# The output product of a memory-recurrent attention in column pieces: one kernel, one change

## The chip, the cores and the metric

The kernel runs on one core of a Trainium2 chip. The metric is the device time of one execution in microseconds; the median of the runs counts. Lower is better. The engines are TensorE (PE, its weight loads PEld), VectorE (DVE), ScalarE (ACT), GpSimd (POOL) and the queue of SyncE (SP), which issues nearly all DMAs. Each engine works through its own instructions in order and waits on semaphores.

## What is computed

Two attentions read the same x (2048 rows of 512) and are mixed by a gate. A goes through 64 segments of 32 rows. Each segment sees 8 memory rows ahead of its own, and the memory rows that it puts out are the next segment's. B is an attention in four blocks of 512 with a linear memory. The reference, cut to what matters:

```python
for s in range(n_seg):                       # 64 segments, seg_len = 32, M = 8
    xs = x[:, s * seg_len:(s + 1) * seg_len, :]
    h = jnp.concatenate([mem, xs], axis=1)   # 40 rows
    q = jnp.einsum('btd,dhe->bhte', h, Wq)   # H = 32 heads of 128; k and v likewise
    ...
    p = _softmax(jnp.where(mask, scores, -1e9), axis=-1)
    o = jnp.einsum('bhqk,bhke->bhqe', p, v)
    o = jnp.einsum('bhte,hed->btd', o, Wo)   # 4096 -> 512
    mem = o[:, :M, :]                        # goes into the next segment
    outs.append(o[:, M:, :])
...
out = g * a + (1 - g) * b                    # g = sigmoid((x * gate_w).sum(-1))
```

## The kernel before

The program first computes B's projections for the first three blocks (up to 50 us of the profiled execution), while the weights of A arrive. Then a part follows, here called the memory part, in which the 64 segments run one after the other, and the rest of B's work fills the gaps.

A segment has 40 rows, and TensorE works on 32 columns of weights by four side by side. So the kernel takes 32 rows as the segment's own: the 8 memory rows and the first 24 rows of x (tile `hT`, the copy of the 24 rows by POOL in `x_copy`, L1555). The last 8 rows of four segments do not depend on the memory and are handled together as one "left" group of 32 rows (`xL`, `left_units`, 16 groups). Keys, queries and values of a left group are put beside those of its segments.

A tile of TensorE of 32 output columns (`pb[bk][SEG * j:SEG * (j + 1)]`, j = 0 to 3) is called a column tile here; four matmuls on the four column tiles run side by side. The steps of a segment are units with short names in a list:

- `K0x K0y K1x ... V1y`: projections (`proj`, L1305), half of the heads (b = 0, 1) and half of the contraction each: 8 matmuls of 512 columns. `k0 q0 v0 ...` evict them (`evac`, L390 on ScalarE or L392 on VectorE), `TK`, `TQ` turn keys and queries on VectorE (`flip`, L1317).
- `S` scores (L1598, L1603), `X` exponential on ScalarE (L1612), `Y` mask on VectorE (L1616), `M` sums (L1633), `L` reciprocal as logarithm and exponential on ScalarE (L1640, L1643), `N` normalization on VectorE (L1647), `n` that of the left columns on POOL (L1653).
- `PV0 PL0`, `PV1 PL1`: value products of each half of the heads, 16 matmuls of 40 columns (L1663) and 4 over the left rows (L1675). They use four row tiles of 32 contraction rows (`tile_position=(SEG * j, 0)`), and each half takes four PSUM banks. `E0a E0b E1a E1b` evict them into `OT_sb`.
- `W0a ... W1b`: product with Wo (`out_part`, L1392). Column tile j takes the heads 4k + j, all 512 outputs each, so that the four tiles hold four partial sums over 8 heads each.
- `H0`, `H1`: eviction of the partial sums as f32 (`WF`), `F0`, `F1`: a product with the f32 matrix `fold` (L1410) that adds the four partial sums and turns the result, so that features lie along the partitions. `hm` copies the 8 memory columns into the next `hT`, `ax` the other columns into `aT_st`.
- The left groups have `ol` units (the same product over `OTL`, 16 of them) and `of` (fold). `os` turns `aT_st` on VectorE and stores it (`aTd`), and the tail units `tb`, `tf` load 128 finished rows, mix them with B's and write them out.

Among these stand B's units: `bS` scores (L933, row tiles too), `bE` exponential (L954), `bP` value products (L986), `bT` what comes after them, `pj`, `pp` late projections of the last block.

The order of the work is written out: sixteen lists `A_LIST0` to `A_LIST15`, one for each four segments. A unit appends its instructions to its engines' streams when its name comes up; semaphore waits follow from what is read and written. A `~` behind a name swaps ScalarE and VectorE in its eviction. Names that end in `e` end a unit begun earlier. PSUM banks are given out in the order of the list (`Banks`), and a bank's new writer waits for its last reader. DMAs stand in SP's queue in the same order.

Of the kernel before, what the change touches and what calls it, by code (L numbers as in the profile page):

```python
# [42 lines left out]
class Banks:  # L43
# [3 lines left out]
    def __init__(self, res):  # L47
        self.free = list(range(len(res)))
        self.res = res
        self.oldest = True  # L50
        self.relief = lambda: False

    def take(self, long=False):
        while not self.free and self.relief():
            pass
        assert self.free, "out of banks"
        f = self.free
        if long:
            c = [b for b in f if b < 2] or f
        elif self.oldest:  # L60
            c = [b for b in f if b > 1] or f
        else:
            whole = [b for b in f if b > 1 and b ^ 1 in f]
            c = [b for b in f if b not in whole and b > 1] if len(whole) <= 4 else [b for b in f if b > 1]
            c = c or [b for b in f if b > 1] or f
        b = c[0]
        f.remove(b)
        return b

    def pair(self):  # L70

        found = lambda: [(max(self.free.index(b), self.free.index(b + 1)), b) for b in self.free if b % 2 == 0 and b + 1 in self.free]
        while not found() and self.relief():
            pass
        c = found()
        c = [x for x in c if x[1] > 1] or c
        assert c, "no two neighbouring banks"
        b = min(c)[1]
        self.free = [k for k in self.free if k not in (b, b + 1)]
        return [b, b + 1]  # L80
# [177 lines left out]
def build(nc, es, A_x, A_mem0, A_Wq, A_Wk, A_Wv, A_Wo, B_wq, B_wk, B_wv, B_wo, B_beta, gate_w, out, dbg=None):  # L258
# [31 lines left out]
    def alloc(stack, *specs):  # L290
        at, spans = 0, {}
        for name, shape, dt, n in specs:
# [10 lines left out]
    alloc(es, ("ident", [128, 128], BF16, 0), ("xT", [128, C, S], BF16, 0), ("hT", [128, C, SEG], BF16, 2),  # L303
          ("Wk_sb", [128, C, HE], BF16, 0), ("Wq_sb", [128, C, HE], BF16, 0), ("Wv_sb", [128, C, HE], BF16, 0),
          ("Wo_sb", [128, H, DM], BF16, 0), ("woB_sb", [128, C, DM], BF16, 0),
          ("gw_sb", [128, C], BF16, 0), ("g_sb", [128, NTT], F32, 0), ("omg_sb", [128, NTT], F32, 0),
# [6 lines left out]
          ("aTg", [128, C, 128], BF16, 0), ("fold", [128, SEG], F32, 0), ("VNL", [128, 2, 512], BF16, 0),  # L313
          ("WF", [128, DM], F32, 0))
# [6 lines left out]
    v.x_sb = v.Wo_sb[:, 0:NTT, :]  # L321
    v.wvB = v.woB_sb
# [7 lines left out]
          ("oTt", [128, 16, 32], F32, 0), ("t1_sb", [128, DM], F32, 0), ("aT_st", [128, C, 128], BF16, 2))  # L330
# [11 lines left out]
    dram("aTd", [NG, 128, DM])  # L342
# [4 lines left out]
    def Rs(name):  # L347
        if name not in R:
            R[name] = Res(name)
            home = v.home(name)  # L350
            if home:
# [5 lines left out]
             ("QT", "QT_sb"), ("VN", "V_sb"), ("Pn", "P_sb"), ("P0", "P_sb"), ("P1", "P_sb"), ("R0", "R_sb"), ("R1", "R_sb"), ("OTL", "OTL"),  # L357
             ("OT", "OT_sb"), ("oTt", "oTt"), ("t1", "t1_sb"), ("aT", "aT_st"))

    def late_home(name):  # L360
        if name.startswith(("aTd", "aTg", "PT")):
            return None
        h = next((t for p, t in homes if name.startswith(p)), None)
        if h in ("KTL", "QTL", "VL", "OTL"):
            h += name[len(h)]
        return h + name[3] if h == "aT_st" else h
# [27 lines left out]
    v.g_out = [P.group("out%d" % i, "out") for i in range(NG)]  # L394

# [32 lines left out]
    v.BK.oldest = False  # L428
    v.BK.free = sorted(v.BK.free)
    plan_a(v, NSEG_RUN)  # L430
    for go in v.g_out:
        if go.count:
            P.ops["sp"].append(Op("sp", (lambda go=go: (lambda sp: sp.wait_ge(go.sem, 16 * (go.base + go.count))))(), [], "final_wait_" + go.name))
# [7 lines left out]
def plan_const(v):  # L441
# [29 lines left out]
    def late():  # L471
# [7 lines left out]
        rf = Rs("fold")  # L479
        gp(lambda g: g.memset(v.fold[:], 0.0), rf, "fold0", True)  # L480
        for j in range(4):
            sel(v.fold[:], [[-1, SEG]], ALU.not_equal, 1.0, -SEG * j, 1, rf, "fold1_%d" % j)
# [17 lines left out]
def plan_warm(v):  # L500
    P, Rs, BK = v.P, v.Rs, v.BK
    v.warm = v.WF[:, :].bitcast(BF16)[:, 0:512]
# [12 lines left out]
def plan_loads(v, A_x, A_mem0, A_Wq, A_Wk, A_Wv, B_wq, B_wk, B_wv, B_wo, B_beta, gate_w):  # L515
# [35 lines left out]
    def wo(q):  # L551
        P.dma(v.grp("Wo%d" % (q // 2)), lambda s: s.dma_start(v.Wo_sb[:, 4 * q:4 * q + 4, :], wosrc[:, 4 * q:4 * q + 4, :]),
              writes=[Rs("Wo%d" % (q // 2))] + ([Rs("x_sb%d%d" % (q, h)) for h in range(2)] if q < 4 else []), name="dma_Wo%d" % q)
# [70 lines left out]
def gate_parts(v):  # L624
# [4 lines left out]
    def dots(k):  # L629
# [4 lines left out]
        def f_gate(pe):  # L634
            ins = None
            for i in range(4 * k, 4 * k + 4):
                for c in range(C):
                    ins = pe.matmul(v.pb[bk][:, i:i + 1], v.xT[:, c, i * 128:(i + 1) * 128], v.gw_sb[:, c:c + 1],
                                    start=(c == 0), stop=(c == C - 1), skip_group_check=True)
            return ins  # L640
        P.op("pe", f_gate, reads=x_res(v, k) + [Rs("gw")], writes=[v.rbank[bk]], name="gate_mm%d" % k)
        if k == NTT // 4 - 1:
            sigmoid(v, v.pb[bk][:, 0:NTT], v.g_sb, v.omg_sb, "g", [v.rbank[bk]])
            BK.give(bk)

    def memory():
# [8 lines left out]
        v.evac("dve", v.hT[0][:, :, 0:v.M], v.pb16[bk][:, 0:C * v.M].rearrange("p (c t) -> p c t", t=v.M), [bk], [Rs("hTm0_0"), Rs("hTm0_1")], "memT0")  # L655
# [133 lines left out]
class LateB:  # L789
# [25 lines left out]
    def project(self):  # L815
# [23 lines left out]
        P.op("pe", f, reads=x_res(v, v.NB - 1) + [Rs("wvB" if m == "V" else "woc%d" % (k % 4))], writes=[v.rbank[bk]], name="lp%d_%d" % (k, half))  # L839
# [4 lines left out]
    def finish(self):  # L844
# [9 lines left out]
        if k == 0:  # L854
            P.op("gp", lambda g: g.memset(self.vst[:, :, 16:17], 1.0), writes=[Rs("t1")], name="v17l")
# [3 lines left out]
                  self.vst[:, :, 0:16].rearrange("p (e m) d -> p m e d", e=2), "t1", "vd%d_%d" % (sb, i)),  # L859
# [9 lines left out]
class BAttn:  # L869
# [45 lines left out]
    def scores(self):  # L915
# [8 lines left out]
        bks = v.BK.pair() + v.BK.pair()  # L924
# [134 lines left out]
A_LIST0 = """  # L1059
    ixl wl 0.Q0x iKL0x iQL1x iQL0x 0.K0x 0.Q0y iQL0 0.K1x 0.K1y 0.q0 0.TQ0 iKL0 0.xc iQL0e 0.K0y iKL0e~ iKL1x 0.k1 bS wl bE bE bE iQL1 wl bE 0.k0~ iKL1 pj  # L1060
    iQL1e 0.qt 0.TK1 iVL1x iVL1 iVL0x iVL0 xl bP iVL0e pj bP iKL1e~ 0.TK0 0.Q1x iVL1e~ QL0x pp QL0 QL0e wl 0.Q1y bS VL0x wl bE VL0 0.V0x wl wl pj iVLt
    0.q1~ bE 0.S0 bE pj KL1x 0.TQ1 bE 0.X0 0.Y0 0.S1 KL0x 0.X1 0.Y1 bP wl 0.V0y VL0e~ 0.M1 0.v0 bP 0.L1 0.N1 0.M0 KL1 KL0 pp VL1x VL1 KL1e KL0e~ bS 0.n1
    pj pj 0.L0 0.N0 QL1x QL1 0.n0 VL1e~ bE bE 0.V1x 0.V1y bE QL1e bE 0.v1~ 0.PV0 1.qt 0.PL0 0.E0a 0.E0b~ 1.xc pj bP 0.PV1 0.PL1 0.E1a~ 0.W0b 0.E1b~ 0.W0a
    0.oL 0.W1a bT 0.W1b pp 0.H0~ bP bS 0.F0 0.H1~ bE 0.hm0 0.ax0 pj 0.F1 0.hm1~ 1.Q0x 1.K0x 1.K0y bE bE 1.k0 0.ax1~ 1.TK0 1.Q0y 1.q0~ 1.TQ0 bE 1.K1x 1.K1y
    1.Q1x 1.Q1y 1.k1 bP 1.TK1 1.S0 1.q1 1.TQ1 1.X0 1.Y0 1.V0x 1.V0y 1.v0 pp 1.S1 1.X1 1.Y1 1.M0 1.V1x 1.V1y 1.L0 1.n0 2.qt 1.N0 1.M1 1.L1 bP 1.n1 pj 1.v1
    1.N1 1.PV0 2.xc 1.PL0 1.E0b~ 1.E0a pj 1.PV1 pp 1.PL1 1.E1b~ 1.E1a~ 1.oL 1.W0a 1.W0b 1.W1b 1.W1a 1.H0 bS 1.F0 bE 1.hm0 1.H1~ 1.F1 2.Q0x 2.K0x 1.hm1~
    1.ax1 2.K0y 2.k0~ 2.TK0 2.Q0y 2.K1x 2.K1y 2.Q1x bE 2.Q1y bE bE 2.q0~ 2.TQ0 2.S0 bP 1.ax0 bP 2.k1~ 2.TK1 2.q1 2.TQ1 2.X0 2.Y0 bS 2.V1x 2.V1y 2.S1 bT
    2.M0 bE VLt bE 2.X1 2.Y1 2.V0x 2.V0y 2.L0 2.n0 2.N0 2.v0~ pj 2.v1 2.M1 2.L1 2.n1 2.N1 3.qt pj 2.PV0 2.PL0 2.E0b~ 2.E0a bE pj pj 2.PV1 2.PL1 2.E1a~ pp
    pp 2.E1b~ 2.oL 2.W0a 2.W0b bT bE 2.W1a 2.W1b 2.H0 3.xc bS bP 2.H1~ bP 2.F0 2.hm0 2.F1 3.K0x 2.ax0 3.Q0x bE bE 2.hm1~ 3.Q0y 3.K0y bE 2.ax1~ bE 3.q0
    3.k0 3.TQ0 3.K1x 3.K1y 3.TK0 3.Q1x 3.S0 3.X0 3.Q1y 3.q1 3.V0x 3.k1~ 3.TK1 3.Y0 3.TQ1 3.V0y 3.v0 3.M0 3.L0 3.n0 3.N0 3.V1x 3.S1 3.V1y bP 3.X1 3.Y1 bP  # L1070
# [813 lines left out]
```

## Time and profile before

| what | us |
|---|---|
| runs | 831.55, 832.46, 835.6 (median 832.46) |
| span of the profiled execution, from its first to its last instruction | 828.9 |
| PE busy | 804.7 |
| DVE busy | 575.6 |
| ACT busy | 592.2 |
| POOL busy | 287.6 |

The profile is of one execution. Of that execution the instruction span is recorded, 828.9 us; the time of a run also holds what lies around the instructions. Matmuls are pipelined: a matmul's recorded time runs from its first read to a modelled end, and matmuls that follow each other overlap. How fast TensorE works is therefore read from the distance between starts. A row of the profile's groups gives line, engine, operation, tiles written and read, shapes, count, busy time, the mean time of one in ns, and the idle time before them with what ended it.

### The profile page before, as it was taken

The page shows a single profiled execution, that of the slowest core. Times are in us where ns is not written, and L with a number is a line of the kernel's source. Part 1 is how long each engine was busy: PE and PEld are TensorE (multiplying, and loading weights), DVE is VectorE, ACT ScalarE, POOL GpSimd, SP SyncE. Part 2 cuts the span into 40 slices and gives each one's busy share as a digit, 9 for nine tenths or more (in the row PEclk, how much of TensorE's full clock was granted, in tenths as well). Part 3 has the DMA queues.
Part 4 walks back from the last instruction along what each step waited for, and adds up shares of the span by engine and source line. Part 5 has one row for each costly group of instructions (what it writes and reads, how often), then busy time and mean ns, then how long its engine had stood idle before and what let it go on. Part 6 is the DMA issues. An engine that isn't in the chain of part 4 may idle for free.

```text
span 828.9 us, 49046 instructions
## 1 busy us (share of the span) xinstructions
PE 804.7 (97%) x21947; PEld 433.6 (52%) x21947; DVE 575.6 (69%) x1392; ACT 592.2 (71%) x1510; POOL 287.6 (35%) x780
## 2 busy tenths in 40 slices
PE   8998999999999999999999999999999999999998
PEld 4544555555445555555555555554555555555544
DVE  4555666577677777687777777877777777677656
ACT  5557777777776867777777777677777686777654
POOL 4613333433333333434342333433333333334111
PEclk9999999999999999999999999999999999999999
DMA  8997312212011121111102121211102111210111
GB/s 329 419 374 223 87 36 62 47 26 60 19 38 36 31 50 27 44 37 47 38 19 46 30 50 32 47 38 46 37 21 50 27 49 33 47 36 17 43 27 47
DMA packets 98257, 57.48 MB, mean 69 GB/s; under 512 B 71800, under 2 KB 92160, under 8 KB 96512
## 3 DMA queue, kind: packets, MB, share of 16 engines
q1 hardware_dynamic: 97488, 53.58, 22.3%
q8 instruction: 172, 2.82, 1.4%
q10 hardware_dynamic: 560, 0.79, 0.3%
q14 instruction: 37, 0.30, 0.1%
HBM read 37.14 MB, written 17.20 MB: 66 GB/s over the span
## 4 chain that ended last, share of the span: by engine, by line
PE 81%; ACT 7%; DMA 5%; DVE 3%; issue 1%; POOL 1%; SPq 0%; ACTq 0%; DVEq 0%; POOLq 0%
PE ps L1305 44%; PE ps L1392 17%; PE ps L1410 4%; PE ps L1663 3%; PE ps L933 2%; PE ps L986 2%; DMA scr_mzd<-MZ 2%; PE ps L1505 2%; DMA scr_kqd<-stgk 2%; PE ps L1598 2%; PE ps L1633 1%; ACT PT L954 1%; PE ps L699 1%; ACT R_sb L1643 1%; ACT WF L390 1%
## 5 line engine op out<-in xcount | busy, mean ns | idle before, releaser
L960 POOL TENSOR_SCALAR_AFFINE_SELECT PT<-PT 128x128 bf16<-128x128 bf16 (+2 forms) x320 | 117.3, 367 | 204.5 <-ACT PT L954 163.5
L954 ACT ACTIVATE PT<-ps 128x512 bf16<-128x512 f32 x320 | 176.1, 609 | 5.8 <-PE ps L933 3.9
L1305 PE MATMUL ps<-Wq_sb,hT 128*32 128x512 bf16 x2048 | 139.4, 379 | 0.5
L1305 PE MATMUL ps<-Wv_sb,hT 128*32 128x512 bf16 x2048 | 137.6, 379 | 0.1
L1305 PE MATMUL ps<-Wk_sb,hT 128*32 128x512 bf16 x2048 | 136.9, 379 | 0.2
L1392 PE MATMUL ps<-Wo_sb,OT_sb 128*32 128x512 bf16 x2048 | 127.4, 380 | 0.0
L1653 POOL TENSOR_TENSOR P_sb<-P_sb,R_sb 128x64 bf16<-128x64 bf16 x128 | 50.9, 398 | 144.8 <-ACT R_sb L1643 140.9
L390 ACT ACTIVATE OT_sb<-ps 128x320 bf16<-128x320 f32 x167 | 67.9, 434 | 22.8 <-PE ps L1675 21.7
L1305 PEld LDWEIGHTS ps<-Wk_sb,hT 128*32 128x32 bf16 x2048 | 59.7, 97 | 45.8 <-ACT hT L390 2.6
L1305 PEld LDWEIGHTS ps<-Wq_sb,hT 128*32 128x32 bf16 x2048 | 59.3, 97 | 45.8 <-ACT hT L390 2.3
L1317 DVE STREAM_TRANSPOSE QT_sb<-QN_sb 128x256 f32<-128x256 f32 x128 | 56.1, 440 | 24.2 <-ACT QN_sb L390 22.0
L1392 PEld LDWEIGHTS ps<-Wo_sb,OT_sb 128*32 128x32 bf16 x2048 | 48.1, 96 | 45.7 <-ACT OT_sb L390 6.4
L1317 DVE STREAM_TRANSPOSE KT_sb<-KN_sb 128x256 f32<-128x256 f32 x128 | 55.9, 439 | 21.6 <-ACT KN_sb L390 18.8
L390 ACT ACTIVATE QN_sb<-ps 128x512 bf16<-128x512 f32 x83 | 49.9, 602 | 28.4 <-PE ps L1305 27.5
L390 ACT ACTIVATE WF<-ps 128x256 f32<-128x256 f32 x97 | 32.8, 381 | 51.6 <-PE ps L1392 51.5
L1612 ACT ACTIVATE P_sb<-ps 128x224 bf16<-128x224 f32 x128 | 45.9, 360 | 27.8 <-PE ps L1603 17.2
L390 ACT ACTIVATE KN_sb<-ps 128x512 bf16<-128x512 f32 x79 | 47.0, 599 | 25.7 <-PE ps L1305 24.8
L1305 PEld LDWEIGHTS ps<-Wv_sb,hT 128*32 128x32 bf16 x2048 | 50.7, 95 | 27.6 <-issue 1.3
L392 DVE CAST OT_sb<-ps 128x320 bf16<-128x320 f32 x89 | 42.9, 488 | 26.0 <-PE ps L1675 25.5
L392 DVE CAST V_sb<-ps 128x512 bf16<-128x512 f32 x82 | 55.9, 683 | 4.0 <-PE ps L1305 3.1
L1647 DVE TENSOR_TENSOR P_sb<-P_sb,R_sb 128x160 bf16<-128x160 bf16 x128 | 42.2, 329 | 20.1 <-ACT R_sb L1643 18.4
L1663 PEld LDWEIGHTS ps<-P_sb,V_sb 32*128 32x128 bf16 x2048 | 23.0, 91 | 54.4 <-DVE P_sb L1647 27.9
(139 smaller groups left out, 1484.7 us busy)
## 6 DMA issues: line engine op xcount, KB each, us to landing
Wk_sb<-in_A_Wk_dram SPq DMA_DIRECT2D x4, 1024.0 KB, 9.8
Wq_sb<-in_A_Wq_dram SPq DMA_DIRECT2D x4, 1024.0 KB, 13.7
Wv_sb<-in_A_Wv_dram SPq DMA_DIRECT2D x4, 1024.0 KB, 16.6
Wo_sb<-in_A_Wo_dram SPq DMA_DIRECT2D x8, 512.0 KB, 6.1
scr_vld<-VNL SPq DMA_DIRECT2D x16, 256.0 KB, 2.3
VL<-scr_vld SPq DMA_DIRECT2D x64, 64.0 KB
scr_kqd<-stgk SPq DMA_DIRECT2D x12, 256.0 KB, 9.6
Vj<-scr_vd SPq DMA_DIRECT2D x32, 68.0 KB, 2.4
```

Source lines behind the costliest of these rows:

```text
L390: P.op("act", lambda a: a.activation(dst, src, ACT.Copy), reads=[v.rbank[k] for k in bks], writes=dres, name=name)
L392: P.op("dve", lambda d: d.tensor_copy(dst, src), reads=[v.rbank[k] for k in bks], writes=dres, name=name)
L954: P.op("act", lambda a: a.activation(pt, v.pb[bk], ACT.Exp, scale=v.SCALE_B), reads=[v.rbank[bk]], writes=[rp], name="be%d_%d" % (n, t))
L960: P.op("gp", lambda g: g.affine_select(mv, mv, [[0, len(cut)], [1, 128]], ALU.is_ge, 0.0, base=0, channel_multiplier=-1), reads=[rp], writ ...
L1305: ins = pe.matmul(pb[bk][SEG * j:SEG * (j + 1), :], lhs(c), cols(w, j) if split else w[:, 512 * j:512 * (j + 1)], start=(c == 0), stop=(c ...
L1317: P.op("dve", lambda d: d.transpose(to, src), reads=reads, writes=writes, name=name)
L1392: ins = pe.matmul(pb[bk][SEG * j:SEG * (j + 1), :], lhs(4 * k + j), Wo_sb[:, 4 * k + j, :], start=(first and k == ks[0]), stop=False, skip ...
L1410: ins = pe.matmul(pb[bk][SEG * j:SEG * (j + 1), SEG * n:SEG * (n + 1)], cols, v.fold[:, :], start=True, stop=True, skip_group_check=True)
L1612: P.op("act", lambda a: a.activation(P_sb[:, b, :], pb[bk][:, 0:224], ACT.Exp, scale=SCALE), reads=[rbank[bk]], writes=[Rs("P%d" % b), Rs( ...
L1647: P.op("dve", lambda d: d.tensor_tensor(wide(P_sb, b)[:, :, 0:L], wide(P_sb, b)[:, :, 0:L], R_sb[:, b, :].rearrange("p (i q) -> p i q", q= ...
L1653: P.op(ENG["n"], lambda d: d.tensor_tensor(left(P_sb), left(P_sb), grp04(R_sb[:, b, :]), ALU.mult), reads=[Rs("R%d" % b)], writes=[Rs("P%d ...
L1663: ins = pe.matmul(pb[bks[j]][:, L * i:L * (i + 1)], V_sb[SEG * j:SEG * (j + 1), b, i * E:(i + 1) * E], P_sb[SEG * j:SEG * (j + 1), b, LW * ...
```

## The change

Wo. Column tile j now takes outputs of its own, 128 of the 512 (64 of each half of the features, `parts`), over all 32 heads: 128 matmuls of 128 columns in four units `W0` to `W3` of 8 heads each, and no partial sums are left. The f32 matrix `fold`, its products and the evictions `WF` are gone. For the next segment VectorE turns the 32 rows straight out of PSUM into `tt` and copies the 8 memory rows of all features (`hm`). The rows are evicted once as bf16 (`WN`, unit `H`) and stored a segment at a time (`ws`); a tail unit `T<g>.l` loads 128 rows in 8 DMAs. The left groups do the same (`O<g>.0` to `.3`, `.e`, tile `OLN`). The last segment is mixed and written from its own turned layout, with its gate in a 17th column.

Value products. `PV` is one unit for both halves: 32 matmuls, then 8 over the left rows, into four banks, each evicted by one of `E0` to `E3`. It waits for both halves' normalization and values.

Memory rows. x lies in `xTp` with 8 columns ahead, so that the segment's 32 rows are one slice of it: the memory rows are written over the last 8 rows of the segment before, after `xL` and the late projections of B have read them. `hT` and POOL's copies are gone.

The list. One list `A_ORDER` of all units takes the place of the sixteen; each unit is named in full, and what was ended on its own when banks ran out has a name of its own. The bank that has been free longest is taken; four banks need not be neighbours. Wo is loaded in the order 0, 4, 1, 5, 2, 6, 3, 7.

```diff
-        whole = [b for b in f if b > 1 and b ^ 1 in f]
...
+        c = [b for b in f if (b < 2) == long] or f
...
+    def four(self):
+
+        return [self.take() for _ in range(4)]
...
+    v.xT = v.xTp[:, :, M:S + M]
...
-    def out_part(bk, ks, first, lhs, reads, name):
+    def parts(ap, j):
+
+        return ap.rearrange("p (a j c) -> p j a c", a=2, j=4)[:, j]
+
+    def out_part(bk, k, first, lhs, reads, name):
 
         def f(pe):
             ins = None
-            for k in ks:
+            for n in range(8):
+                h = 16 * (n // 4) + 4 * k + n % 4
                 for j in range(4):
-                    ins = pe.matmul(pb[bk][SEG * j:SEG * (j + 1), :], lhs(4 * k + j), Wo_sb[:, 4 * k + j, :],
-                                    start=(first and k == ks[0]), stop=False, skip_group_check=True)
+                    ins = pe.matmul(pb[bk][SEG * j:SEG * (j + 1), 0:128], lhs(h), parts(Wo_sb[:, h, :], j),
+                                    start=(first and not n), stop=False, skip_group_check=True)
...
-    def fold(bk, hf, part, res, name):
-
-        def f(pe):
-            ins = None
-            for n in range(2):
-                for j in range(4):
-                    cols = by_pairs(part[:, :])[:, 2 * hf + n, SEG * j:SEG * (j + 1)]
-                    ins = pe.matmul(pb[bk][SEG * j:SEG * (j + 1), SEG * n:SEG * (n + 1)], cols, v.fold[:, :],
-                                    start=True, stop=True, skip_group_check=True)
...
+            for r in range(3 if last else 4):
+                P.dma(grp, lambda sp, r=r: sp.dma_start(rows[SEG * r:SEG * (r + 1) - M], v.aTd[4 * g + r].rearrange("(j t) (a c) -> t a j c", j=4, a=2)[M:SEG]),
+                      reads=[Rs("aTd%d" % (4 * g + r))], writes=[Rs("aTg")], name="lda%d_%d" % (g, r), scratch=True)
...
-    def x_copy(s):
-        P.op("gp", lambda gq: gq.tensor_copy(hT[s % 2][:, :, M:SEG], xT[:, :, SEG * s:SEG * (s + 1) - M]),
-             reads=x_all, writes=[Rs("hTx%d" % (s % 2))], name="hx%d" % s)
-
     def segment(s):
...
+        lhs = lambda c: xTp[:, c, SEG * s:SEG * (s + 1)]
...
-        def pv_main(b):
-            bks = held[b] = B.pair() + B.pair()
+        def values():
+            bks = held[0] = B.four()
 
             def f_main(pe):
                 ins = None
-                for i in range(4):
+                for b in range(2):
+                    for i in range(4):
+                        for j in range(4):
+                            o = 4 * L * b + L * i
+                            ins = pe.matmul(pb[bks[j]][:, o:o + L], V_sb[SEG * j:SEG * (j + 1), b, i * E:(i + 1) * E],
+                                            P_sb[SEG * j:SEG * (j + 1), b, LW * i:LW * i + L], start=(i == 0 and b == 0), stop=False,
+                                            tile_position=(SEG * j, 0), skip_group_check=True)
...
+        def w_mem():
+            src = pb[wb["bk"]][:, 0:128].rearrange("p (a q n) -> p a n q", a=2, n=2)
+            P.op("dve", lambda d: d.transpose(v.tt[:, :, :].rearrange("p (a n) t -> p a n t", a=2), src), reads=[rbank[wb["bk"]]], writes=[Rs("tt")], name="hmT%d" % s)
+            dst = xTp[:, :, SEG * (s + 1):SEG * (s + 1) + M]
+            P.op("dve", lambda d: d.tensor_copy(dst, v.tt[:, :, 0:M]), reads=[Rs("tt")], writes=[Rs("xt%d" % (s + 1))], name="hm%d" % s)
...
+                evac(ENG["H0"], WN[:, :], pb[wb["bk"]][:, 0:128], [wb["bk"]], [rw], "wev%d" % s)
...
+        def w_rows():
+            rows_out(v.aTd[s], WN[:, :], [rw], Rs("aTd%d" % s), P.group("as%d" % s, "as%d" % (s % 2)), "sta%d" % s)
```

A stretch of the new list, from one segment's value products to the next one's first projections (`L7` is the left group of segments 28 to 31, `O5` the left group's product, `T4` a tail):

```text
25.PV L7.QL0x bT O5.e 25.E0 25.E1~ 25.W0 25.W1 26.qt 25.E2 25.W2 25.E3~ 25.W3 25.hm bT L7.KL1y L7.QL0y 26.K0x
```

867 lines of the change are left out of this document (336 added, 531 removed).

## The prediction

> **What bounds the kernel now.** I read the shares of busy time first, then the chain, then the order of time on TensorE.
>
> ```profile
> PE 804.7 (97%) x21947; PEld 433.6 (52%) x21947; DVE 575.6 (69%) x1392; ACT 592.2 (71%) x1510; POOL 287.6 (35%) x780
> ...
> PE 81%; ACT 7%; DMA 5%; DVE 3%; issue 1%; POOL 1%; SPq 0%; ACTq 0%; DVEq 0%; POOLq 0%
> ```
>
> TensorE is busy 97% of the span, at the full granted clock in all 40 slices, and carries 81% of the chain; no other engine passes 71%. So I price the change in TensorE time. "Busy" includes the overlap of pipelined matmuls, so durations (379 ns) are no prices. Prices are distances between starts, read in the timeline of TensorE (columns: start, time, line, count).
>
> ```profile
> 406.06 0.27 PE L1598 MATMUL ps<-QT_sb,KT_sb 128*32 128x40 bf16 x16
> 406.16 0.21 PE L1603 MATMUL ps<-QT_sb,KTL 128*32 128x32 bf16 x8
> 406.21 0.60 PE L1305 MATMUL ps<-Wv_sb,hT 128*32 128x512 bf16 x8
> ...
> 407.17 0.28 PE L986 MATMUL ps<-PT,Vj 128*32 128x256 bf16 x4
> 407.28 0.27 PE L1633 MATMUL ps<-P_sb,onesb 128*32 128x160 bf16 x8
> 407.38 1.04 PE L1305 MATMUL ps<-Wk_sb,xL 128*32 128x512 bf16 x16
> ...
> 408.48 0.21 PE L1675 MATMUL ps<-P_sb,VL 32*128 32x64 bf16 x4
> 408.62 0.29 PE L986 MATMUL ps<-PT,Vj 128*32 128x256 bf16 x4
> ...
> 409.86 1.91 PE L1392 MATMUL ps<-Wo_sb,OT_sb 128*32 128x512 bf16 x32
> 411.70 0.40 PE L933 MATMUL ps<-QTj,KTj 32*128 32x128 bf16 x12
> ```
>
> Four small matmuls on the four tiles run side by side; I call them a quad. A quad of 512 columns is followed by the next after 216 ns (the Wo product: 32 matmuls in 1.84 us, with a switch at its end), of 256 after 110, of 160 and 64 together 100 (407.28 to 407.38), of 40 or 32 after 25 (16 in 100 ns). Weights of 32 rows by 128 ("32*128", the row form) behave otherwise: L1675's one quad takes 0.14 us (408.48 to 408.62). Over all starts of the trace, the last quad before a row-form stretch is 105 ns longer at least, the last of the stretch 95.
>
> From the first matmul of the memory part at 50.0 us the trace then splits so. Quads of 512: 2692 x 216 ns = 581.5 us. Fold: 2560 records x 8 ns = 20.5. Scores and main value products: 1280 x 25 = 32.0. Sums 12.4, left values 3.6, B attention 17.5 + 18.8, rest 1.1. That is 687.4. The 206 row-form stretches cost 206 x 0.20 = 41.2. What is left of the 775.7 us is waiting, **47.1 us**: before the value products 11.6 and within them 4.9, before the next segment's projections 10.8, before the fold 5.3, before Wo 1.3, others 13.2. With 50.0 ahead and 3.1 behind, this is the span of 828.8; the median of the runs, 832.46, lies 3.6 above it.
>
> **The change, part by part.**
>
> *Fold gone.* 20.5 us of matmuls go (1280 instructions, each two records).
>
> ```profile
> L1392 PE MATMUL ps<-Wo_sb,OT_sb 128*32 128x512 bf16 x2048 | 127.4, 380 | 0.0
> L1410 PE MATMUL ps<-fold,WF 128*32 128x32 f32 x2048 | 37.7, 199 | 6.0 <-ACT WF L390 2.2 <-ACT hT L390 1.1 <-issue 0.9
> L986 PE MATMUL ps<-PT,Vj 128*32 128x128 bf16 x256 | 9.4, 219 | 0.0
> ```
>
> *Wo in pieces of 128.* A segment had 8 quads of 512 (1.73 us); it gets 32 quads of 128. L986 has that very form (128x32 weights, 128 columns): its first quad is followed by the next after 56 ns (32 cases, 55 to 57). So 1.79 us, +64 ns in each of 64 segments and 16 left groups: **+5.1**. Bounds: 53 ns (a quarter of 216, no fixed part), which gives -2.6, and 94 ns (PEld is busy 48.1 us for 2048 Wo loads, 23.5 each, four in a row), which gives +102. I take 56, the same form; the 16 loads that go with 16 scores in 100 ns speak against 94.
>
> *Value products in one unit.* The instruction orders of the two kernels have 206 and 139 row-form stretches: 67 x 0.20 = **-13.4**.
>
> *VectorE turns the memory rows.* ScalarE loses WF (38.0), hT (16.7) and aT (19.7), gains about 13 in WN and OLN and 5 elsewhere: near 536 us. VectorE loses about 47, gains 63 turns, 63 copies and 33 small evictions, about 44: near 567. POOL loses 18.0. None comes near TensorE. The turn of 128x128 from PSUM is not in the trace:
>
> ```profile
> L1317 DVE STREAM_TRANSPOSE KT_sb<-KN_sb 128x256 f32<-128x256 f32 x128 | 55.9, 439 | 21.6 <-ACT KN_sb L390 18.8
> ...
> L1010 DVE STREAM_TRANSPOSE oTt<-ps 128x512 f32<-128x512 f32 x56 | 39.6, 707 | 7.0 <-PE ps L1036 5.1 <-PE ps L986 0.6
> ...
> L1323 DVE STREAM_TRANSPOSE KTL<-LN_sb 128x128 f32<-128x128 f32 x64 | 25.2, 408 | 4.9 <-ACT LN_sb L390 3.4
> ```
>
> By slope from 512 to 256 it is 0.30 us; L1323 of its size, with a scattered target, 0.41; L1010 is the far end, 0.71. I take 0.36. A tenth more costs up to 6 us.
>
> *Waits in the new list.* For each wait I set the time that must pass against the TensorE work that the list of units puts in between, at the paces above, switches included.
> - Sums to value product: 1.37 us (eviction 0.30, exponential 0.34, product 0.33, hand-overs; seen from 820.54 to 821.91). Before 128 places lack 11.2 us; after 64 places lack 13.3.
> - Value product to Wo: 0.68 (0.23 until the eviction starts, 0.44, 0.11, less the switch). Before 5.3. After, 43 of 64 segments have 0.45 or less there: 13.7.
> - Wo to the next segment: before, eviction 0.72 (lacks 11.9) and fold to projection 0.50 (9.0). After, 0.22 + 0.36 + 0.05 + 0.17 + 0.11 = 0.91 against a median of 0.66: 17.8. Behind the waiting turn VectorE holds evictions, but TensorE waits for it first.
>
> The method gives 37.4 for before, where the trace has 29.0 on these links (78%). So 44.8 after becomes about 35. The other 18.1 lose half of the 4.9 within value products, 2.5, leaving 15.6: **50.5 us of waits, +3.4**. Bounds: 29 (all three links at 30% of the method's figure, about what the trace has before Wo, 1.3 of 5.3) and 78 (all as computed, and 0.71 for the turn, which adds 18).
>
> *At nothing.* The 64 row copies on POOL (0.28 each) lie beside TensorE's other work; POOL waits most of the span, and if that cover fails nothing is lost, as they go. The 63 stores of WN, 16 of OLN and 126 loads that replace 60 stores and 15 loads stand in SP's queue ahead of KTj, QTj, Vj and VL loads (1.9 to 2.4 us to land). They are hidden by lists that issue those loads a job ahead; a load that came 2 us late at each of the 16 groups would cost 32. Code: 27069 matmuls for 20669. Bank choice changes which eviction a unit waits for; that is in the 15.6.
>
> *End.* After the last Wo product before runs fold, eviction, transpose and a mix, some 3.1 us beyond priced matmuls; after, 0.22 + about 0.35 + 2.1 = 2.7.
>
> Sum: 50.0 + matmuls 672.0 (687.4 - 20.5 + 5.1) + switches 139 x 0.20 = 27.8 + waits 50.5 + end 2.7 = 803.0, and 3.6 around it: **807 us**.
>
> **The rivals.**
> 1. *Weight loads show* (slower). Each Wo quad needs four loads, and a 128-column quad hides only 56 ns of them against 216. At 94 ns a quad, 2560 x 38 ns = 97 us more: 904. The gain of about 25 is gone from 66 ns a quad on. For it: it was never so dense for 128 matmuls on end. Against: L986 at 56, and loads in the scores every 6 ns. Chance 0.05. [...]
> 2. *The code isn't there in time* (slower). The instruction queue moved 2.82 MB in 172 packets for 44,195 TensorE records, 64 bytes each, so one Wo unit of 256 takes a whole packet in 1.79 us. In the trace a packet takes 0.9 to 1.8 us and none start closer than 3.3. One such packet late by 1 us in 80 units: 887. Chance 0.03. [...]
> 3. *The chain decides.* Waits of 78 to 95, as VectorE is late for the turn behind other work: 834 to 851, at their lower end no change. Chance 0.09.
> 4. *The list hides more*: waits under 29, so under 785. Chance 0.07.
> 5. *The change doesn't do what it says*: both orders show the counts, so only the paces can fail, which is 1.
>
> **How the numbers follow.** Forecast 0.76, rivals 0.05, 0.03, 0.09, 0.07. The range is the forecast's own with waits of 29 to 78: 785 to 834, which leaves about 0.16 out. Half a per cent is what a measurement of this kernel can tell: faster below 828.3 and slower above 836.6. Of the forecast 0.74 lies below 828.3, and rival 4: faster 0.81. Same 0.06. Slower 0.13, being most of 3, and 1 and 2.
>
> **What would show it.** Wo quads of 128 columns every 56 ns (1.8 us for the 128 of L1338) confirm the second step; 66 or more refute it. No f32 matmul is left. Stretches in row form number 139. Waits before the first projection of a segment (for the VectorE copy) near 14 us, before Wo (for the first eviction) near 11, before value products near 10; if these sum to 60, the method is too kind. The turn takes 0.30 to 0.41. VectorE stays under 75% busy. The prediction is wrong if the unlisted waits, which I carry over, depend on the list.

## The result and the profile after

| | before | after |
|---|---|---|
| median of the runs, us | 832.75 (831.55 to 835.6, 4 runs) | 924.61 (920.3 to 926.05, 4 runs) |
| ratio | | 1.110, 95% interval 1.106 to 1.113 |
| span of the profiled execution, us | 828.9 | 924.3 |
| PE busy / not busy, us | 804.7 / 24.2 | 806.7 / 117.6 |

The kernel became 11% slower; the forecast was 807 with a range of 785 to 834. First the shares of busy time, the granted clock in 40 slices, the instruction queue and the chain of the kernel after:

```profile
PE 806.7 (87%) x27067; PEld 474.8 (51%) x27067; DVE 564.7 (61%) x1370; ACT 547.4 (59%) x1276; POOL 265.3 (29%) x711
...
PEclk9998999999999999999999999999999999999989
...
q8 instruction: 212, 3.47, 1.5%
...
PE 71%; issue 9%; DMA 5%; ACT 5%; DVE 4%; SPq 3%; POOL 2%; POOLq 0%; DVEq 0%; ACTq 0%
```

TensorE is as busy as before, yet 93 us longer not busy. No other engine took its place (VectorE fell from 69% to 61%). What grew is "issue", from 1% of the chain to 9%: time in which TensorE waited for nothing that the profile records. The groups say where (busy us, mean ns, then idle time ahead and what ended it):

```profile
L1338 PE MATMUL ps<-Wo_sb,OT_sb 128*32 128x128 bf16 x8192 | 139.6, 223 | 49.4 <-issue 46.9
...
L1578 DVE STREAM_TRANSPOSE tt<-ps 128x128 f32<-128x128 f32 x63 | 20.0, 317 | 120.6 <-PE ps L1338 120.5
```

The Wo products have 46.9 us of "issue" inside them, where before the same row had 0.0. VectorE's turn takes 0.317 us. The timeline of TensorE shows what the 46.9 us look like:

```profile
407.23 1.34 PE L1338 MATMUL ps<-Wo_sb,OT_sb 128*32 128x128 bf16 x83
408.99 0.84 PE L1338 MATMUL ps<-Wo_sb,OT_sb 128*32 128x128 bf16 x45 [0.42 <-issue]
...
421.04 1.73 PE L1338 MATMUL ps<-Wo_sb,OT_sb 128*32 128x128 bf16 x109
423.69 0.46 PE L1338 MATMUL ps<-Wo_sb,OT_sb 128*32 128x128 bf16 x19 [0.92 <-issue]
```

One run of 128 products is cut in two by a hole, after 83 products in one segment and after 109 in another, though nothing in the program stands there. To find what the places share, I numbered TensorE's records in the trace (weight loads, products, its own event records) in order of start. Of the idle times above 0.3 us, 69 with 70.8 us together lie ahead of record numbers that leave the same remainder, 193, when divided by 256; all others together make 30.5 us. Before, one such hole has that remainder (0.9 us). And 256 instructions of 64 bytes are one packet of the instruction queue (3.47 MB in 212 packets of 16,384 bytes each, for 54,352 TensorE records). In the trace the packets' starts are never closer than 3.29 us, a tenth of the distances are below 3.45, and the median is 3.88 (before 4.53). Each of the 69 holes ends 1.2 to 1.6 us after such a packet has ended. So the theory that I tested is the second rival's, with another price: **TensorE's code comes at most 256 instructions in about 3.4 us, 13 ns each, and a Wo of 256 instructions in 1.79 us, 7 ns each, runs out of it.** Against it stood: the weight loads slow each 128-column quad alike (the first rival), and the new list with its waits makes the time.

### The profile page after: what moved, and what is told of

Read it like the earlier page. It is cut to its first block, busy times and chain, and to the rows that moved or that the text cites. A ratio compares the mean times of both kernels' runs of the same rounds, so it can differ in the third digit from the quotient of the medians.

```text
span 924.3 us, 58945 instructions
## 1 busy us (share of the span) xinstructions
PE 806.7 (87%) x27067; PEld 474.8 (51%) x27067; DVE 564.7 (61%) x1370; ACT 547.4 (59%) x1276; POOL 265.3 (29%) x711
## 3 DMA queue, kind: packets, MB, share of 16 engines
q8 instruction: 212, 3.47, 1.5%
## 4 chain that ended last, share of the span: by engine, by line
PE 71%; issue 9%; DMA 5%; ACT 5%; DVE 4%; SPq 3%; POOL 2%; POOLq 0%; DVEq 0%; ACTq 0%
PE ps L1251 39%; PE ps L1338 16%; PE ps L917 2%; PE ps L1541 2%; PE ps L970 2%; POOL PT L944 2%; PE ps L1510 1%; DMA scr_kqd<-stgk 1%; PE ps L1477 1%; PE ps L683 1%; DMA scr_vld<-VNL 1%; ACT PT L938 1%; ACT R_sb L1520 1%; PE ps L821 1%; SPq L1292 1%
## 5 line engine op out<-in xcount | busy, mean ns | idle before, releaser
L938 ACT ACTIVATE PT<-ps 128x512 bf16<-128x512 f32 x320 | 173.6, 601 | 87.6 <-PE ps L917 63.9
L1338 PE MATMUL ps<-Wo_sb,OT_sb 128*32 128x128 bf16 x8192 | 139.6, 223 | 49.4 <-issue 46.9
L1338 PEld LDWEIGHTS ps<-Wo_sb,OT_sb 128*32 128x32 bf16 x8192 | 122.1, 99 | 74.0 <-issue 54.7
L1251 PE MATMUL ps<-Wk_sb,xTp 128*32 128x512 bf16 x2048 | 144.6, 386 | 10.2 <-issue 3.7
L1251 PE MATMUL ps<-Wq_sb,xTp 128*32 128x512 bf16 x2048 | 143.2, 385 | 5.0 <-issue 3.6
L1251 PE MATMUL ps<-Wv_sb,xTp 128*32 128x512 bf16 x2048 | 142.6, 379 | 0.0
L373 ACT ACTIVATE OT_sb<-ps 128x320 bf16<-128x320 f32 x172 | 64.8, 439 | 48.8 <-PE ps L1552 48.2
L1578 DVE STREAM_TRANSPOSE tt<-ps 128x128 f32<-128x128 f32 x63 | 20.0, 317 | 120.6 <-PE ps L1338 120.5
L1251 PEld LDWEIGHTS ps<-Wq_sb,xTp 128*32 128x32 bf16 x2048 | 57.8, 98 | 63.9 <-issue 13.5
L1251 PEld LDWEIGHTS ps<-Wk_sb,xTp 128*32 128x32 bf16 x2048 | 56.2, 97 | 66.4 <-issue 10.1
L1251 PEld LDWEIGHTS ps<-Wv_sb,xTp 128*32 128x32 bf16 x2048 | 47.1, 95 | 21.2 <-issue 1.5
L1495 DVE TENSOR_TENSOR P_sb<-P_sb,mkeep 128x224 bf16<-128x224 bf16 x128 | 36.1, 282 | 25.1 <-ACT P_sb L1491 22.6
```

The costliest lines, as they stand in the source:

```text
L373: P.op("act", lambda a: a.activation(dst, src, ACT.Copy), reads=[v.rbank[k] for k in bks], writes=dres, name=name)
L938: P.op("act", lambda a: a.activation(pt, v.pb[bk], ACT.Exp, scale=v.SCALE_B), reads=[v.rbank[bk]], writes=[rp], name="be%d_%d" % (n, t))
L1251: ins = pe.matmul(pb[bk][SEG * j:SEG * (j + 1), :], lhs(c), cols(w, j) if split else w[:, 512 * j:512 * (j + 1)], start=(c == 0), stop=(c ...
L1338: ins = pe.matmul(pb[bk][SEG * j:SEG * (j + 1), 0:128], lhs(h), parts(Wo_sb[:, h, :], j), start=(first and not n), stop=False, skip_group_ ...
L1495: P.op(ENG["y"], lambda d: d.tensor_tensor(P_sb[:, b, :], P_sb[:, b, :], mkeep[:, :], ALU.min), reads=[Rs("mkeep")], writes=[Rs("Pm%d" % b ...
L1578: P.op("dve", lambda d: d.transpose(v.tt[:, :, :].rearrange("p (a n) t -> p a n t", a=2), src), reads=[rbank[wb["bk"]]], writes=[Rs("tt")] ...
```

## The experiments

| kernel | what it is | median, us | ratio to before, 95% | PE not busy, us |
|---|---|---|---|---|
| e1_wide | after, Wo in 512 columns | 833.79 | 0.9995 to 1.0033 | 51.5 |
| e2_mid | after, half of Wo in 256 columns | 841.75 | 1.0056 to 1.0119 | 55.1 |
| e3_split | before, Wo in 128 columns | 995.25 | 1.1876 to 1.2016 | 141.6 |
| e5_spread | after, list changed | 946.92 | 1.1353 to 1.1413 | 136.5 |
| e6_onepv | before, value products in one unit | 909.53 | 1.0866 to 1.0958 | 97.8 |
| e7_noe | e1, Wo waits for no eviction | 831.74 | 0.9978 to 1.0001 | 50.9 |
| e11_nomem | e7, memory rows not copied | 824.02 | 0.9851 to 0.9928 | 46.3 |
| e9_cut | e11, value products wait for no norm | 819.11 | 0.9796 to 0.9865 | 45.7 |
| e10_vlt | e1, one load earlier | 831.99 | 0.9967 to 1.0008 | 50.9 |
| e12_vl2 | e1, that load ahead of Wo's | 837.16 | 1.0009 to 1.0061 | 48.8 |

The two kernels of bursts, e4 and e8, ran once each and have no time to compare; they are read from their traces.

### Fewer instructions for the same columns

```diff
 e1_wide, in out_part of the kernel after
-            for n in range(8):
-                h = 16 * (n // 4) + 4 * k + n % 4
+            for n in range(2):
                 for j in range(4):
-                    ins = pe.matmul(pb[bk][SEG * j:SEG * (j + 1), 0:128], lhs(h), parts(Wo_sb[:, h, :], j),
+                    h = 16 * n + 4 * k + j
+                    ins = pe.matmul(pb[bk][SEG * j:SEG * (j + 1), :], lhs(h), Wo_sb[:, h, :],
 e2_mid: for n in range(4), h = 16 * (n // 2) + 4 * k + n % 2, and
+                    ins = pe.matmul(pb[bk][..., 0:256], lhs(h), Wo_sb[:, h, 256 * (j % 2):256 * (j % 2) + 256],
```

> The kernel after, but a unit of Wo is again 8 heads in 2 groups of 4 products of 512 columns (one head on each column tile), and the four partial sums are not added: the addition of the column tiles is left out, the rest of the computation, the units, the list, the turn by VectorE stay as in the kernel after. 6144 pairs of load and product fewer than after. Code theory (TensorE's code comes in packets of 256 instructions, one in 3.35 us at best, and a Wo of 256 instructions runs out of it): the holes of about 1 us in the Wo units go, 800 to 812 us. Weight theory (a group of four 128-column products costs about 109 ns instead of 56 wherever it stands): the same 800 to 812 us, so this run does not part these two. List theory (the new list of units, its waits and VectorE's turn make the time): stays at 900 us or more.

> The kernel after, but a unit of Wo is 16 products of 256 columns in place of 32 of 128: half of the heads are left out of Wo, the rest stays. The columns that stream are as many as after (4 groups x 110 ns = 0.44 us a unit against 8 x 56 ns = 0.45 us), the instructions half as many. Code theory: 128 instructions in 1.76 us are 13.75 ns each, just slower than the packets come (13.1 ns each), so most holes go: 808 to 840 us. Weight theory: a load hides behind 256 columns, 803 to 815 us. List theory: the TensorE time wanted is the same as after's, so 915 to 930 us.

e1_wide took 833.79 us: the 92 us over the kernel before are gone with the pieces, and so are the holes (none above 0.3 us at remainder 193). Its span is 94.0 us below after's. Its page:

```profile
PE 778.8 (94%) x19387; PEld 378.4 (46%) x19387; DVE 565.0 (68%) x1370; ACT 546.4 (66%) x1276; POOL 264.7 (32%) x711
...
L1338 PE MATMUL ps<-Wo_sb,OT_sb 128*32 128x512 bf16 x2048 | 123.2, 382 | 2.6 <-ACT OT_sb L373 1.9
```

But it is 22 us above the upper end of what both the code and the weight theory wanted, so a second cause is left; I come to it below. e2_mid streams as many columns as after's Wo (4 groups of 256 a unit against 8 of 128) in half of the instructions, and took 841.75, just past the 808 to 840 of the code theory and 83 below after. Three holes with 1.6 us are left at the boundaries. Together these two refute that the new list makes the 92 us, but do not part code from weight loads.

### The same pieces in the old kernel

```diff
 e3_split, in out_part of the kernel before
-                for j in range(4):
-                    ins = pe.matmul(pb[bk][SEG * j:SEG * (j + 1), :], lhs(4 * k + j), Wo_sb[:, 4 * k + j, :],
+                for c in range(4):
+                    for j in range(4):
+                        ins = pe.matmul(pb[bk][SEG * j:SEG * (j + 1), 128 * c:128 * c + 128], lhs(4 * k + j), Wo_sb[:, 4 * k + j, 128 * c:128 * c + 128],
```

In this kernel each of the four pieces of the first product begins a sum anew, so the output is not the reference's; the work is the same.

> The kernel before with its list, its fold and its results, but each Wo product of 512 columns is cut into four of 128 columns (the same weights loaded again each time): 2048 groups of four in place of 512, as many as after has. Code theory: a Wo of 64 groups grows from 13.8 us-worth of columns per 8 groups to as many columns in four times the instructions; 8 groups at 216 ns become 32 at 56 ns in stream time, holes at packet boundaries of about 1 us, +75 to +105 us: 908 to 938 us. Weight theory: +53 ns x 2048 = +108 us, 941 us, without holes, each group alike at about 109 ns. List theory: 2048 groups at 56 ns against 512 at 216 ns, +4 us: 835 to 842 us.

It took 995.25 us, 162 more than before; no theory expected so much. The groups show why:

```profile
L1393 PE MATMUL ps<-Wo_sb,OT_sb 128*32 128x128 bf16 x8192 | 144.1, 222 | 58.6 <-issue 58.5
...
L1411 PE MATMUL ps<-fold,WF 128*32 128x32 f32 x2048 | 40.0, 202 | 21.8 <-issue 16.5 <-ACT WF L390 1.5 <-ACT PT L954 1.5
```

Behind Wo stands the fold, whose records follow each other every 8 ns (2560 of them in 20.5 us, before): with code already late from Wo it starves as well. The holes at packet boundaries hold 116.4 us in 90 cases: 69.4 on Wo, 24.3 on the fold. The old list with its waits is kept here, so the pieces alone do this. My +75 to +105 left out the fold; without it the holes hold 92 us. Another 41 us are not holes: TensorE's busy time is 845.7 us against 804.7, at a mean clock of 0.983; I did not split them.

### Bursts on TensorE alone

```python
# e4_burst: n columns, pairs of load and product, on tile i % 4
for n, pairs in ((512, 256), (128, 768), (512, 256), (32, 768), (512, 256), (256, 768), (512, 256), (160, 768), (512, 128)):
    for i in range(pairs):
        j = i % 4
        pe.matmul(pb[bk][32 * j:32 * j + 32, 0:n], w[:, 32 * j:32 * j + 32], w[:, 0:n], start=True, stop=True)
```

> A kernel that leaves out the whole computation (its output is zeros): TensorE alone runs bursts of pairs of load (128x32) and product on four column tiles, on zeros, nothing else running: 768 pairs of 128 columns, 768 of 32, 768 of 256, 768 of 160, parted by 256 pairs of 512 columns. 768 pairs are 1536 instructions, six packets. Code theory: the bursts of 128, 32 and 160 columns take nearly the same time, 14 to 20 us each (six packets at 3.35 us, less what was fetched ahead during the 512-column burst), with a hole once in every 128 pairs and groups of four at about 56 ns and 25 ns between the holes; the burst of 256 columns takes 192 x 110 ns = 21.1 us with hardly a hole. Weight theory: no holes; groups of 128 and of 32 columns both at about 109 ns, 20.9 us a burst, 256 columns at 110 ns. If neither holds (the cost comes from other work beside TensorE): 10.8 us for 128 columns, 4.8 us for 32, 13.4 us for 160, no holes.

The three dense bursts took 20.2 us (128 columns), 19.0 (32) and 20.1 (160), and 256 columns 21.0. The timeline in the burst of 128 columns:

```profile
17.73 4.04 PE L469 MATMUL ps<-aTg 128*32 128x512 bf16 x232
23.32 1.97 PE L469 MATMUL ps<-aTg 128*32 128x128 bf16 x128 [1.54 <-issue]
26.77 1.97 PE L469 MATMUL ps<-aTg 128*32 128x128 bf16 x128 [1.48 <-issue]
30.50 1.97 PE L469 MATMUL ps<-aTg 128*32 128x128 bf16 x128 [1.76 <-issue]
34.23 1.97 PE L469 MATMUL ps<-aTg 128*32 128x128 bf16 x128 [1.76 <-issue]
38.23 2.29 PE L469 MATMUL ps<-aTg 128*32 128x128 bf16 x60 [2.03 <-issue]
```

A hole stands after exactly 128 pairs each time, 3.45 to 4.0 us from one to the next, and the first after 216 pairs of the burst. The burst of 32 columns has its holes after the same 216, 344, 472, ... pairs and takes nearly the same time, though its columns are a quarter as many. Between the holes the quads of 128 columns are 55.7 ns apart, those of 32 columns 33, of 160 69. In the burst of 256 columns there is no hole. Here nothing waits for anything, VectorE and GpSimd are busy for 0.00 us from 20 to 38 us, and DMAs move 5 GB/s. So the weight loads are not what slows a quad, and the code theory's mechanism is shown.

```python
# e8_mix, quads: A 64 of 512; B 128 of 128, then 64 of 512; C 64 times (two of 128, one of 512)
# D 256 row-form of 256, then 256 of 512; E 64 times (four row-form of 256, four of 512)
```

> Leaves out the whole computation (output zeros): TensorE alone, on zeros, in stretches: A 64 groups of four 512-column products; B 128 groups of 128 columns, then 64 of 512; C the same groups mixed, two of 128 then one of 512; D 256 row-form groups of 256 columns, then 256 column-form groups of 512; E the same in turns of four and four. Code theory: B takes 24 to 27 us with two or three holes at packet boundaries, C takes 21.0 us (64 x 0.328) with none, since 24 instructions in 0.328 us are 13.7 ns each. Without that limit B and C take 21.0 us both. Switch price: E is longer than D by 64 x (105 + 95 ns) = 12.8 us if the prices of the prediction hold; equal if a switch of form is free.

B took 26.4 us with three holes of 1.4 to 1.8 us, C 21.08 with none: the same quads in another order, 5.3 us apart. D took 83.8 us, E 97.3: 13.5 us for 64 times into the row form and out, 0.211 us each. So the prediction's 0.20 us a stretch holds.

### Other work between the pieces

If order cures it, fill could be moved between the pieces. e5_spread takes 102 half units of the left groups from where the list of after had them and puts them between W0, W1, W2 and W3, for instance:

```diff
-    2.W0 2.W1 2.W2 3.qt pp~ 2.W3
+    2.W0 L1.VL0y 2.W1 L1.QL1y 2.W2 3.qt pp~ 2.W3
```

> The kernel after with its results; only its list is changed: 102 of the half units of the rows that span two segments (8 pairs of 512 columns each, 16 instructions in 0.43 us) are moved to stand between W0, W1, W2 and W3 of segments 1 to 58. Code theory: 16 instructions come in 0.21 us and take 0.43, so each that stands in front of a late packet shortens the hole by up to 0.22 us, 102 of them by up to 22 us in all: 900 to 916 us, and the idle time in holes at packet boundaries (71.6 us in 74 holes over 0.3 us in the kernel after) falls to 50 to 62 us. List theory (the waits of the list make the time, and these moves take work out of where the list had put it): 924 us or more.

The holes at packet boundaries fell from 70.8 to 44.5 us, more than I had reckoned (0.22 us for each moved half gives 22). But the time rose by 22 us to 946.92, as the other idle times above 0.3 us went from 30.5 to 62.0. The code theory's holes moved as it says; its forecast of the time failed, as I read it because fill that closes a hole is missing where it covered a wait, and there it was worth more. So these moves do not cure it.

### The value products alone, and the links behind them

e6_onepv is the kernel before with `PV1 PL1` doing both halves as in the kernel after, `PV0 PL0` taken out and the evictions of the first half moved behind it; lists and fold stay.

> The kernel before with its results, its fold and its lists, with one part of the change alone: the value products of both halves of a segment in one unit, at the second one's place, with the four evictions behind them. 64 row-form stretches fewer. As the prediction priced it (0.20 us a stretch, the links behind it covered): 818 to 824 us. If the links behind the one unit stand open (in e1_wide TensorE waits 10.1 us in front of Wo where the kernel before waits 1.3, and 28.0 in front of value products against 16.5): 826 to 845 us.

It took 909.53 us, far outside both forecasts, with no more than 1.8 us of holes at packet boundaries. The group of Wo tells it:

```profile
L1230 PE MATMUL ps<-Wo_sb,OT_sb 128*32 128x512 bf16 x2048 | 129.4, 388 | 47.4 <-ACT OT_sb L390 23.7 <-DVE OT_sb L392 21.5 <-ACT LN_sb L390 2.1
```

In the old lists PV1 stood between PV0 and the first Wo and covered the eviction. With one unit nothing stands there, and by the distances of starts TensorE waits 52.6 us in front of Wo, 0.82 in each segment, against 1.3 us in all before. So the one unit saves 64 x 0.2 = 13 us by its price and costs 51 at this link. By difference another 38 us of the span (905.2 against 828.9) are lost elsewhere, before value products and projections among others; the mean clock of 0.992 is a part of them. The list has to put other work between; the new one does so, and in e1_wide 10.1 us are left there.

### What is left in e1_wide

By the prediction's sum e1_wide should span 803.0 - 5.1 = 797.9 us; it spans 830.3. Busy times of TensorE in four stretches (columns: stretch, length, busy time of PE and count, the other engines, the granted clock, DMA), e1_wide first and the kernel before second:

```profile
0.00:50.00 50.00, 45.79 (x392) 25.58 (x393) 24.04 (x52) 27.79 (x50) 21.00 (x96) 1.00 0.98 378
50.00:100.00 50.00, 38.72 (x871) 17.70 (x872) 24.48 (x57) 24.28 (x54) 11.37 (x30) 0.93 0.59 187
100.00:700.00 600.00, 581.92 (x15276) 282.29 (x15268) 435.75 (x1065) 417.02 (x989) 198.84 (x501) 1.00 0.18 42
700.00:830.00 130.00, 112.42 (x2864) 52.80 (x2860) 80.72 (x197) 77.35 (x184) 33.52 (x84) 0.97 0.15 35
```

```profile
0.00:50.00 50.00, 46.29 (x379) 25.94 (x379) 23.96 (x52) 27.78 (x50) 22.72 (x103) 1.00 0.97 378
50.00:100.00 50.00, 46.12 (x1170) 23.20 (x1168) 29.25 (x69) 33.98 (x78) 14.50 (x40) 1.00 0.68 206
100.00:700.00 600.00, 588.85 (x16840) 317.71 (x16836) 434.96 (x1054) 446.14 (x1161) 215.27 (x552) 1.00 0.16 39
700.00:828.00 128.00, 123.41 (x3576) 66.76 (x3568) 87.46 (x218) 84.32 (x223) 35.11 (x86) 1.00 0.15 37
```

Not busy: 11.3 against 3.9 us from 50 to 100, 18.1 against 11.2 in the 600 us of the middle, 17.9 against 5.5 from 700 to the end (the ends of the spans are at 830.3 and 828.9). Of 27.3 us more, 20 lie at the two ends; that the list has little to put in between there is my reading. At the start one wait stands out, in e1_wide:

```profile
PE ps L1552 <- DMA VL<-scr_vld: 7.8, 1, 7.8
```

It is 6.7 us in the kernel after and 1.9 before. Two kernels move that load:

```diff
 e10_vlt
-    ... L0.VL0e~ wl L0.VL1e 0.Q0x ... 0.M0 wl L0.VLt 0.V0x
+    ... L0.VL0e~ wl L0.VL1e L0.VLt 0.Q0x ... 0.M0 wl 0.V0x
 e12_vl2: the first three wl stay, then
+    ... L0.VL0e~ L0.VL1e L0.VLt wl wl wl wl wl 0.Q0x ...
```

> e1_wide with one token of the list moved: the load of the first group's values of spanning rows (L0.VLt) stands right behind L0.VL1e, ahead of two of the eight Wo loads. In e1_wide and in the kernel after TensorE waits once for this load, about 7 us at 75 us, in the kernel before 1.9 us. If that wait is the order of the loads: 826 to 830 us. If Wo is then late in its place, or the values' own store is what lands late: 832 to 836 us.

> e1_wide (no addition of the column tiles) with a few tokens of the list's start moved: the store and the load of the first group's values of spanning rows go ahead of five of the eight Wo loads. In e1_wide the store is issued at 62.3 us behind six Wo loads and lands at 71.3, and TensorE waits 7.8 us for the load that follows. If the order of the transfers makes that wait: it falls below 3 us, 826 to 830 us. If the transfers as a whole are late (Wo then lands late in its place): 831 to 836 us.

e10 took 831.99 us against e1's 833.79, too close to call a gain, and TensorE still waits 8.4 us. In e12 the wait for it is 3.1, and Wo is late instead:

```profile
PE ps L1167 <- DMA Wo_sb<-in_A_Wo_dram: 5.0, 2, 3.3
PE ps L1381 <- DMA VL<-scr_vld: 3.1, 1, 3.1
```

At 837.16 us it is no faster. That does not show that the transfers as a whole are late, for e12 does not have the order of the kernel before. Here is SyncE's queue at that point, e12 first and before second:

```profile
63.53 0.34 SPq L1113 DMA_DIRECT2D scr_vld<-VNL  x1
68.56 2.51 SPq L1121 DMA_DIRECT2D VL<-scr_vld  x4
71.11 3.21 SPq L531 DMA_DIRECT2D Wo_sb<-in_A_Wo_dram  x5
```

```profile
61.42 0.34 SPq L1340 DMA_DIRECT2D scr_vld<-VNL  x1
...
62.28 3.66 SPq L552 DMA_DIRECT2D Wo_sb<-in_A_Wo_dram  x4
66.53 2.71 SPq L1348 DMA_DIRECT2D VL<-scr_vld  x4
```

The load of VL waits for its store, and in e12 the queue issues nothing else from 63.9 to 68.6 us, while before issues four Wo loads between the two. That order was not tried in e1_wide, so the cause of the wait at the start stays open. The kernel before also had more TensorE work ahead of that point (22.0 us busy from 50 to 75, e1_wide 14.5).

Three kernels cut the recurrent chain of e1_wide, one link after the other:

```diff
 e7_noe
-            out_part(wb["bk"], k, first, lambda h: OT_sb[:, h, q], [Rs("OT%d" % k)], ...)
+            out_part(wb["bk"], k, first, lambda h: Wk_sb[:, 0, 32 * h:32 * h + 32], [], ...)
 e11_nomem, also
-            P.op("dve", lambda d: d.tensor_copy(dst, v.tt[:, :, 0:M]), ...)
 e9_cut, also
-                                            P_sb[SEG * j:SEG * (j + 1), b, LW * i:LW * i + L], ...
+                                            onesb[SEG * j:SEG * (j + 1), 0:L], ...
```

> e1_wide, with the segments' Wo reading a slice of Wk in place of the evicted value products, so that it waits for no eviction: the data of the output are other ones, the work is the same; e1_wide left out the addition of the column tiles, so this does. If the open link from the evictions to Wo is worth the 10.1 us that TensorE waits there: 821 to 826 us against e1_wide's 834. If another wait takes its place: 831 to 836 us.

> e1_wide with Wo reading a slice of Wk and the memory rows not copied into x (the value products wait for the normalised probabilities as in e1_wide; no addition of the column tiles). Links alone: 10.1 + 14.4 us less, 808 to 814 us. Other work late in their place: 822 to 832 us.

> e1_wide (no addition of the column tiles) with the recurrent chain cut in three places: Wo reads a slice of Wk, the value products read a constant tile in place of the normalised probabilities, and the memory rows are not copied into x, so that value products, Wo and the next projections wait for nothing of their own segment but V; TensorE's work is the same, VectorE leaves out 63 small copies. If the 80.8 us of waits in e1_wide are the chain's links: those in front of value products (28.0), Wo (10.1) and the next segment's first projections (14.4) go, 52 us less: 778 to 795 us. If other work is late as soon as these are gone (the batch part, scores and sums, whose engines are 65 to 70 per cent busy): 810 to 830 us.

They took 831.74, 824.02 and 819.11 us, each as the second forecast has it, with other work late in place of the link: each cut gains a part of its link (2, then 8, then 5 us of the 52). With the chain cut in all three places TensorE is still 12.4 us not busy from 50 to 100, 13.7 in the middle and 15.9 from 700 on. So the third rival, the chain, is worth about 15 us here, and the two ends stay nearly as they are without it.

## Why the prediction was wrong, point by point

The profiled span is 121.3 us above the sum of 803.0. It splits at e1_wide: 94.0 - 5.1 = 88.9 us belong to the pieces, 830.3 - 797.9 = 32.4 to the rest.

- **"Wo in pieces of 128", +5.1, is the step that failed**: it measures +94.0. Its price, 56 ns a quad, is right as a quad's own pace (55.7 in the burst). I took it from runs of two quads, 16 instructions, and carried it to runs of 32 quads. By the trace's starts the 10,240 products of L1338, with what passes before the next product, take 223.1 us; e1_wide's 2,560, which stream as many columns, take 153.1. That is 70 of the 94 us, and holes of 10.5 us more fall on the projections behind them. The prediction lists the code, 27069 matmuls for 20669, among the terms at nothing and gives no reason there: that is the term that was missing. The bounds of the step (-2.6 to +102) did hold it, by the far end, for another reason than the one given there, and the range of 785 to 834 did not use them.
- **Rival 2 had the mechanism and nearly the size** (80 holes of 1 us, 887 us) at a chance of 0.03. I had written both numbers side by side, a Wo unit takes a packet in 1.79 us and no two packets start closer than 3.3, and did not divide the one by the other: 3.3 us was not slack but the floor of the pace. Before, 44,195 records in the span are 18.8 ns each on average, above 13; the average hid that the dense part would be local. No run ahead of the prediction showed how much code TensorE holds ahead. The burst bounds it: in the stretches of 512 columns ahead of the dense bursts, packets start 6.4 to 7.6 us apart, only as fast as 256 instructions are used up at 27 ns each, so it seems that TensorE had all the code that it can hold; yet the first hole comes some 430 instructions into a burst of 1536. So it held at most those 430, less than two packets of 256: an estimate from these numbers.
- Rival 1, weight loads: refuted by the burst, with 55.7 ns a quad on four column tiles (13.9 a matmul) between the holes, the same as the price of 56, now in runs of 32 quads too. The 109 ns a quad that the expectations give to the weight theory are an assumption, and no run shows them.
- "Fold gone" and "Value products in one unit": e8 has the switch at 0.211 us for my 0.20. In e1_wide TensorE is 25.8 us less busy where these two steps said 33.9; the mean clock of 0.992 (before 1.000) is at most 6.6 us of 830, an estimate, and a part of that falls on idle time. So the gap of 8.1 us is not fully explained; busy time, which counts overlaps, is a rough measure for it.
- "VectorE turns the memory rows": the turn is 0.317 us (0.30 to 0.41 forecast), VectorE busy 564.7 us (567), ScalarE 547.4 (536, 11 too low; ScalarE is 5% of the chain). Right in the main.
- "Waits in the new list", +3.4, measures +27.3 (not busy, e1_wide against before). Two of the three links came out as forecast: by distances of starts e1_wide waits 14.4 us before a segment's first projections (forecast near 14) and 10.1 before Wo (near 11). Before and within the value products it waits 28.0 against some 12.5 (10 and 2.5); 9.2 of them are waits for the load of VL, mostly the one at the start, so that link is about 6 us too low, and in the middle of the span it is +6.9. The larger part lies outside: I had carried "others" over from before, and the start (+7.4) and the end (+12.4) are among them. The prediction named that itself as what would make it wrong. Why the end has 12.4 us more was not tested, and what makes the start late stays open (above).
- Rival 3 (834 to 851) meets the time of e1_wide, 833.8, but not by its mechanism: cutting the chain gives back 15 us, and most of what e1_wide waits stays.

No version here beats the kernel before with the whole computation in it. The pieces would have to come with half the instructions; and e1_wide, with a quarter of them and without any addition of the partial sums, only equals it.

## What to carry to other kernels

Price a TensorE stretch by two floors: its columns and its instructions, here 13 to 15 ns an instruction (3.29 us from packet to packet at the least in the kernel after, 3.88 in the median), counted over each packet of 256 (C of e8, at 13.7 on average in mixed order, has no hole; B has them, and in the kernel after a hole stands inside a run of 128 products). Four matmuls of 256 columns, 110 ns for 8 instructions, just reach it; four of 128 take 56 ns by their columns and some 105 or more by this floor, an estimate from 8 times 13.1. When the smallest distance of two events is the same wherever one looks (3.28 us between packets before, 3.29 after), take it for a rate limit and not for slack. A merged unit removes a switch and the cover of what follows it, and fill moved to one gap opens another: look what stood between.

## What the runs showed that was not expected

- In the burst of 32 columns, with idle times of 2.2 to 2.5 us in each 3.5 to 3.7, the granted clock falls to 0.62 on average (56 to 73 us); in that of 128 columns, with 1.5 to 2.0 us, it stays at 1.00 (20 to 38 us). In the wait of 7.8 us in e1_wide it is 0.72 (70 to 75 us), in the 5 us behind it 0.60, then 1.00.
- The packet's cycle in the dense bursts, from the trace: a packet begins 0.7 to 1.6 us (1.05 in the middle) after the first product of the packet before it has started, takes 0.9 to 1.4 us, and 1.3 to 1.6 us pass from its end to its own first product. These three make up the 3.3 to 4.0 us from hole to hole, so the floor looks like the time of one round and not like a bandwidth: the transfer itself is a third of it. That the start on one packet is what asks for the next is a reading of the trace, not tested.
